# One more group of layer 1 by seven output products instead of eight, in a fused Fourier filter and two-layer MLP

## The chip, the cores and the metric

The kernel runs on one core of a Trainium2 chip. The metric is the device time of one execution in microseconds; three runs of the kernel before gave 1121.1 to 1121.34 us, median 1121.32. In the profile's names PE is TensorE (PEld its weight loads, which overlap the matmuls), DVE is VectorE, ACT is ScalarE, POOL is GpSimd, and SP issues most of the DMAs.

## The reference, cut to what matters

```python
X = np.fft.rfft(x, axis=1)                       # x: 2 x 3008 x 256
Yr = shrink(Xr @ w_r - Xi @ w_i + b_r)           # shrink: towards 0 by 0.01
Yi = shrink(Xr @ w_i + Xi @ w_r + b_i)
x = np.fft.irfft(Yr + 1j * Yi, n=3008, axis=1).reshape(6016, 256)
h = x @ w_in1;  x = (h * sigmoid(1.702 * h)) @ w_out1   # 256 -> 2048 -> 256, "layer 0"
h = x @ w_in2;  return (h * sigmoid(h)) @ w_out2        # the same sizes, "layer 1"
```

The change is in layer 1, and in the part of layer 0 that prepares layer 1's weights.

## The kernel before, in words

**Tiles.** The 6016 tokens lie in columns of `yt`, 256 features on 2 x 128 partitions. A layer goes through six blocks of tokens (five of 2 x 512 columns, the last of 2 x 448). In a block eight groups p = 0 to 7 follow each other, each for 256 of the 2048 hidden features, so a group's input part is a 2x2 by 2x2 product of 128-wide blocks. Every factor is held as a rounded high half (fp32r) and a low half, the remainder, and one product is three matmuls: high by high, and the two mixed ones. So the unit of PE's work is three matmuls.

**Scheme of seven.** The input part takes seven products instead of eight everywhere (`prod`, L1009 in `group`, L1191 in `group7`). The sums of input blocks that it needs are made once a block: two differences by `xsums` (L883, L884), then rounding (L898) and remainder (L905) by `xprep`. In groups 1 to 5 of layer 1 the output part takes seven products too (`s_prod`, L1127): its weights come ready split from DRAM (`stage` writes them in layer 0, `stream` loads 1 MB a group into `ring`), and its factors are the four gated values and the differences t1 = y3 - y1, t3 = b22 - y3, t2 = b22 - t1 (L1264 to L1266) and t4 = t2 - y4 (L1304). Groups 0, 6 and 7 use the plain eight products (`out7`, L1150), group 0 and 7 of them in `group`, not `group7`.

**Order in a group.** The engines run the order of the code. A group's own output products are taken by the next group, between its seven input products. In `group7` the input products are X (0, then 4, then 5, then 2 on one bank, with ACT or DVE reading in between), Y (1) and Z (3, then 6). ACT copies y1 (L1215), y2 (L1228) and y3 (L1230), DVE adds (L1219, L1244, L1246), ACT gates with Silu (L1201) and rounds (L1204), and the low half is subtracted by POOL (L1208; L1235 for factor 4) or by DVE (L1208, factor 2). Factor 3's low half goes by a DMA that adds (L1251). In the next group the output products come as factors 1, 2, 5, 7, 4, 6, 3; those of 5 and 4 go to the tile `r` and DVE adds them up (L1131, L1133), the others accumulate in banks. Factor 4 needs t4, which needs the y4 of the group before.

**Around a block's end.** In group 6 the sums of the seven are put together (`ends`). The four outputs of a block are added to the plain products of groups 6 and 7 by `final` (L1160) in group 0 of the next block, and DMAs issued by SP carry them off. SP also issues the loads of `ring`, one a group.

Of the kernel before, what the change touches and what calls it, by code (L numbers as in the profile page):

```python
# [21 lines left out]
P = 128  # L22
# [12 lines left out]
WEIGHTS += [(kind, 1, p, False) for kind in ("in", "out") for p in range(8)]  # L35
# [21 lines left out]
def spectral_mlp_kernel(ctx, tc, xin, mfwd, minv, wc, bias, w_in1, w_out1, w_in2, w_out2, outT):  # L57
# [186 lines left out]
    def stage(kind, p):  # L244
# [710 lines left out]
    def out_mm(l, i, p, row, h, gh, gl):  # L955
# [25 lines left out]
        if last:  # L981
            for mm in range(2):
                y = yt[:, mm, t0 + h * n : t0 + (h + 1) * n]
                (nc.scalar.copy if mm else nc.vector.tensor_copy)(y, acc[h, mm])
# [11 lines left out]
    def group(l, i, p, hook):  # L996
# [37 lines left out]
        (nc.vector.tensor_copy if (l, i, p) == (1, 0, 0) else nc.scalar.copy)(y1, X)  # L1034
# [80 lines left out]
    def s_prod(i, p, k):  # L1115
# [4 lines left out]
        one, first = k in (4, 5), p == seven(i)[0]  # L1120
        if k == 4 and p == seven(i)[-1]:
# [4 lines left out]
        for m, (st, mv) in enumerate(((a, hi), (z, hi), (a, lo))):  # L1126
            nc.tensor.matmul(t, st, mv, start=m == 0 and (one or first and k not in (2, 3)), stop=m == 2, skip_group_check=True)  # L1127
        if one:
            acc = accs[k][:, :n]
            if first and k == 5:  # L1130
# [6 lines left out]
    def out7(i, p, row, h, gh, gl):  # L1137
# [3 lines left out]
        for mm in range(2):  # L1141
            if p == 0 and row == h:
                for k in (C_BANK[h, mm],) + ((7,) if h and mm else ()):
                    banks[k] = ps_p[0].tile([P, 512], F32, tag="D", name="m3") if k == 3 else bank(1, f"m{k}")
            t = banks[C_BANK[h, mm]][:, :n]
            first = row == h and (p == 0 or p == tail and mm == 1)
# [4 lines left out]
        if p == 0 and row != h:  # L1151
            t = banks[C_BANK[h, 1]][:, :n]
            if h:
                nc.vector.tensor_copy(accs[6][:, :n], t)
            else:
                nc.scalar.mul(accs[4][:, :n], t, -1.0)
        if p == NPR - 1 and row != h:
            def final(mm):
                y = yt[:, mm, t0 + h * n : t0 + (h + 1) * n]
                nc.vector.tensor_add(y, home[("b22", "u", "w", "c22")[2 * h + mm]][:, :n], banks[C_BANK[h, mm]][:, :n])  # L1160
# [16 lines left out]
    def group7(i, p, hook):  # L1177
# [15 lines left out]
        def S(*ks):  # L1193
            for k in ks:
                if s7:
                    s_prod(i, p - 1, k)
                elif k in (1, 2, 7, 3):
                    out7_next()
# [16 lines left out]
        nc.scalar.copy(y1, X)  # L1215
# [9 lines left out]
        if ends:  # L1225
            u1, u2 = (home[x][:, :n] for x in ("b22", "u"))
# [20 lines left out]
        gate(b22, y2)  # L1247
        rounding(3, b22)
        if g7:
            nc.scalar.mul(factor(i, p, 3)[1], b22, -1.0)  # L1250
            nc.gpsimd.dma_start(out=factor(i, p, 3)[1], in_=b22, accum_op=ALU.add)  # L1251
        elif not ends:
            rest(nc.vector, 3, b22, (1, 1))
        if ends:
            add, sub = nc.vector.tensor_add, nc.vector.tensor_sub
            a4, a5, a6 = (accs[k][:, :n] for k in (4, 5, 6))
# [4 lines left out]
        gate(y3)  # L1261
# [13 lines left out]
        if ends:  # L1275
            add(a6, a6, a5)
            add(a5, u2, a5)
            if R3 == 1:
                rest(nc.vector, 3, b22, (1, 1))
                pend[-1], pend[-2] = pend[-2], pend[-1]  # L1280
            add(u2, u2, banks[7][:, :n])
# [34 lines left out]
    moves[0, last, 3].append(("out", 1, 0))  # L1316
# [28 lines left out]
    for at, f, x in (((1, 0, 2, 2), place_tail, 3), ((0, 5, 0, 2), put_aside, 3), ((0, 5, 7, 2), put_aside, 4), ((1, 0, 0, 2), place, 6), ((1, 0, 1, 2), place, 7), ((1, 1, 2, 3), put_back, 3), ((1, 2, 2, 3), put_back, 4)):  # L1345
# [29 lines left out]
    for at, (l, i, p) in enumerate(seq):  # L1375
# [55 lines left out]
        if (l, i, p) == (0, last, 0):  # L1431
            r = cv_p.tile([P, 2 * CU], mybir.dt.int64, tag="raw", name="raw64", bufs=1).bitcast(F32)
            raw64.extend((r[:, : 2 * CU], r[:, 2 * CU :]))
        if (l, i, p) == (1, 0, 0):
# [6 lines left out]
            ring[:] = [m_p.tile([P, MW], F32R, tag="m", name="ring")[:, : 2 * FS * D] for _ in range(2)][::-1]  # L1441
            home.update(zip(("t4", "u", "c22"), spots(3)), w=accs[5])
# [4 lines left out]
        if (l, i, p) == (1, 1, 1):  # L1447
            home.update(zip(("t4", "u", "c22"), spots(0)))
        if (l, i, p) == (1, 2, 1):
# [151 lines left out]
```

## Time and profile before

| | |
|---|---|
| median of three runs | 1121.32 us (1121.1 to 1121.34) |
| the profiled execution | 1124.35 us, of which its span 1122.6 us |
| PE, PEld busy | 1115.1 us (99%), 928.6 us (83%) |
| DVE, ACT, POOL busy | 841.1 us (75%), 831.8 us (74%), 582.1 us (52%) |
| TensorE clock granted | 1.0 of 2.4 GHz throughout |

Shares are averages over the Fourier part (to about 250 us), layer 0 (to about 650 us) and layer 1. A wait is read where it stands: in the idle time of PE's weight loads, and in the order of starts on the engines that make the operands.

### The profile page before, as it was taken

To read this page: it belongs to the slowest core of one execution; us is meant where nothing else is said; L and a number is where in the kernel's file an instruction comes from. 1 tells how busy PE (TensorE), PEld (TensorE's weight loads), DVE (VectorE), ACT (ScalarE), POOL (GpSimd) and SP (SyncE) were. 2 spreads that over 40 slices of the span, in tenths; PEclk is the share of its full clock that TensorE was granted. 3 is DMA by queue.
4 is the path that set the end of the run, shared out by engine and by line. 5 is a ranking of instruction groups with operands and counts; after the bars stand their busy time and mean duration, and the time that the engine had idled before them with its cause. 6 is when DMAs were issued, how large, how long until landed. Compare 5 with 4: busy or idle time off the path is not lost.

```text
span 1122.6 us, 15172 instructions
## 1 busy us (share of the span) xinstructions
PE 1115.1 (99%) x5000; PEld 928.6 (83%) x5000; DVE 841.1 (75%) x1264; ACT 831.8 (74%) x1567; POOL 582.1 (52%) x491
## 2 busy tenths in 40 slices
PE   9999999999999999999999999999999999999998
PEld 6878987888888888888889988888888888788897
DVE  7879997775575576676577787777887877878776
ACT  2488367876676677676678788778888788697785
POOL 0254056444443444434446647657657567477485
PEclk9999999999999999999999999999999999999999
DMA  8699586531121222312424444145054043242341
GB/s 335 167 174 210 148 158 119 118 73 38 38 76 38 54 59 80 108 48 84 120 87 158 153 150 105 47 160 141 10 197 113 19 153 102 76 140 57 121 138 41
DMA packets 54624, 123.87 MB, mean 110 GB/s; under 512 B 5265, under 2 KB 18193, under 8 KB 50578
## 3 DMA queue, kind: packets, MB, share of 16 engines
q1 hardware_dynamic: 36466, 92.44, 23.4%
q0 software_dynamic: 18080, 30.47, 16.9%
q8 instruction: 39, 0.64, 0.2%
q14 instruction: 39, 0.32, 0.1%
HBM read 71.85 MB, written 20.58 MB: 82 GB/s over the span
## 4 chain that ended last, share of the span: by engine, by line
PE 88%; DVE 4%; DMA 3%; issue 2%; ACT 2%; POOL 1%; SPq 0%; POOLq 0%; ACTq 0%; DVEq 0%
PE x L1009 24%; PE o L968 23%; PE x L1191 13%; PE m L1127 9%; PE m L1150 8%; PE r L1127 3%; PE psf L448 3%; PE y L1191 2%; DMA xl<-xt 2%; PE psf L489 1%; DMA x<-yt 1%; PE psm L642 1%; POOL xl L567 1%; DMA raw<-in_x 1%; PE psm L645 0%
## 5 line engine op out<-in xcount | busy, mean ns | idle before, releaser
L1022 POOL TENSOR_TENSOR g<-yt,g 128x512 fp32r<-128x512 f32 (+1 forms) x174 | 231.6, 1333 | 275.4 <-PE x L1009 129.5
L1009 PE MATMUL x<-x,wi 128*128 128x512 f32 (+1 forms) x1260 | 314.2, 387 | 1.4 <-ACT yt L1059 1.3
L968 PE MATMUL o<-g,wo 128*128 128x512 f32 (+1 forms) x1152 | 280.0, 385 | 0.0
L1009 PEld LDWEIGHTS x<-x,wi 128*128 128x128 f32 x1260 | 235.5, 188 | 49.9 <-ACT yt L1059 3.1
L968 PEld LDWEIGHTS o<-g,wo 128*128 128x128 f32 x1152 | 216.3, 188 | 40.3
L1208 POOL TENSOR_TENSOR g<-yt,g 128x512 fp32r<-128x512 f32 (+1 forms) x138 | 189.4, 1389 | 74.2 <-ACT g L1204 63.0
L1012 ACT ACTIVATE yt<-yt 128x512 f32<-128x512 f32 (+1 forms) x180 | 112.1, 623 | 133.7 <-DVE yt L1069 113.9
L1191 PE MATMUL x<-x,wi 128*128 128x512 f32 (+1 forms) x648 | 168.0, 385 | 0.1
L1017 ACT CAST g<-yt 128x512 fp32r<-128x512 f32 (+1 forms) x234 | 144.1, 616 | 6.0
L1191 PEld LDWEIGHTS x<-x,wi 128*128 128x128 f32 x648 | 121.5, 188 | 23.4 <-ACT yt L1230 0.8
L1127 PE MATMUL m<-g,ring 128*128 128x512 f32 (+1 forms) x414 | 111.7, 385 | 0.0
L1204 ACT CAST g<-yt 128x512 fp32r<-128x512 f32 (+1 forms) x186 | 108.0, 613 | 4.2 <-DVE yt L1266 1.1
L1150 PE MATMUL m<-g,wo 128*128 128x512 f32 (+1 forms) x396 | 97.9, 385 | 0.0
L188 POOL DMA_DIRECT2D cv_a<-cv_c x32 | 29.8, 930 | 125.4 <-DVE cv_c L187 105.1
L1127 PEld LDWEIGHTS m<-g,ring 128*128 128x128 f32 x414 | 77.7, 188 | 14.5
L1150 PEld LDWEIGHTS m<-g,wo 128*128 128x128 f32 x396 | 74.3, 188 | 13.9
L1201 ACT ACTIVATE yt<-yt 128x512 f32<-128x512 f32 (+1 forms) x108 | 67.0, 621 | 21.1 <-DVE yt L1244 17.0
L1039 DVE TENSOR_TENSOR yt<-yt,x 128x512 f32<-128x512 f32 (+1 forms) x60 | 40.3, 672 | 42.9 <-ACT yt L1034 42.8
L1069 DVE TENSOR_TENSOR yt<-yt,x 128x512 f32<-128x512 f32 (+1 forms) x60 | 40.4, 674 | 40.2 <-PE x L1009 39.9
L905 DVE TENSOR_TENSOR x<-yt,x 128x512 fp32r<-128x512 f32 (+1 forms) x55 | 47.6, 866 | 28.5 <-ACT x L898 28.4
L1022 DVE TENSOR_TENSOR g<-yt,g 128x512 fp32r<-128x512 f32 (+1 forms) x60 | 41.1, 685 | 31.7 <-ACT g L1017 31.7
L1133 DVE TENSOR_TENSOR raw<-raw,r 128x512 f32<-128x512 f32 (+1 forms) x48 | 32.5, 676 | 31.9 <-PE r L1127 31.9
(211 smaller groups left out, 1845.1 us busy)
## 6 DMA issues: line engine op xcount, KB each, us to landing
ring<-sout SPq DMA_DIRECT2D x30, 1024.0 KB, 5.9
raw<-in_wi SPq DMA_DIRECT2D x32, 256.0 KB, 3.8
cv_a<-cv_c POOLq DMA_DIRECT2D x32, 256.0 KB, 5.3
raw<-in_wo SPq DMA_DIRECT2D x16, 512.0 KB, 3.8
xl<-xt POOLq DMA_DIRECT2D x22, 256.0 KB, 7.1
out_t<-yt SPq DMA_DIRECT2D x20, 256.0 KB, 2.1
raw<-in_x SPq DMA_DIRECT2D x9, 512.0 KB, 6.4
ge<-yt POOLq DMA_DIRECT2D x15, 256.0 KB, 3.8
```

The lines of the kernel that those rows point to most:

```text
L905: E('xl1' if l else 'xl0' if i == 0 else 'xl', k).tensor_sub(lo, src, r32(hi))
L968: nc.tensor.matmul(acc[h, mm], st, mv, start=first and k == 0, stop=last and k == 2)
L1009: nc.tensor.matmul(ps, st, mv, start=first and m == 0, stop=m == 2, skip_group_check=True)
L1012: nc.scalar.activation(g, g if src is None else src, func)
L1017: nc.scalar.copy(gh, g)
L1022: eng.tensor_sub(gl, g, r32(gh))
L1127: nc.tensor.matmul(t, st, mv, start=m == 0 and (one or first and k not in (2, 3)), stop=m == 2, skip_group_check=True)
L1150: nc.tensor.matmul(t, st, mv, start=first and k == 0, stop=k == 2, skip_group_check=True)
L1191: nc.tensor.matmul(ps, st, mv, start=first and m == 0, stop=m == 2, skip_group_check=True)
L1201: nc.scalar.activation(g, g if src is None else src, AF.Silu)
L1204: nc.scalar.copy(factor(i, p, k)[0], src)
L1208: eng.tensor_sub(lo, src, r32(hi))
```

## The change

Group 0 of each block of layer 1 goes through `group7` and the scheme of seven, so seven output products instead of eight are taken in group 1. For that a sixth unit ("out", 0) is split and written to DRAM in layer 0, and `ring` is loaded six times a block instead of five. In group 0 the third difference t3 and factor 3's low half are made by POOL, t2 by DVE in group 1, and two of the four final sums move to group 1 as well. The two sums of `xsums` move from DVE in group 1 to POOL in group 6, and the seventh and fifth inputs (x 6, x 5) are rounded right after the sixth (x 4).

```diff
+WEIGHTS += [("in", 1, 6, False), ("in", 1, 7, False)] + [("out", 1, p, False) for p in range(6)]
...
     def seven(i):
-        return range(1, NPR - 2)
+        return range(NPR - 2)
-    STEPS = ((0, 4), (1, 2), (1, 3), (1, 7), (1, 5), (1, 5))
-    STAGED = {(3, 1): ("in", 6), (3, 3): ("in", 7), (4, 1): ("out", 1), (4, 3): ("out", 2), (5, 0): ("out", 3), (5, 2): ("out", 4), (5, 4): ("out", 5)}
+    STEPS = ((0, 1), (1, 2), (1, 3), (1, 7), (1, 5), (1, 5))
+    STAGED = {(2, 1): ("in", 6), (2, 3): ("in", 7), (3, 1): ("out", 0), (3, 3): ("out", 1), (4, 1): ("out", 2), (4, 3): ("out", 3), (5, 0): ("out", 4), (5, 3): ("out", 5)}
...
     def group7(i, p, hook):
...
         gate(b22, y2)
+        if p == 0:
+            gate(y3)
+        while p and finals:
+            finals.pop()()
         rounding(3, b22)
-        if g7:
+        if g7 and p:
             nc.scalar.mul(factor(i, p, 3)[1], b22, -1.0)
             nc.gpsimd.dma_start(out=factor(i, p, 3)[1], in_=b22, accum_op=ALU.add)
...
         if g7:
             nc.vector.tensor_sub(t1, y3, y1)
-            nc.vector.tensor_sub(t3, b22, y3)
-            nc.vector.tensor_sub(t2, b22, t1)
+            if len(finals) > 1:
+                finals.pop()()
+            if p == 0:
+                nc.gpsimd.tensor_sub(t3, b22, y3)
+                rest(nc.gpsimd, 3, b22)
+                after.append(lambda: nc.vector.tensor_sub(t2, b22, t1))
...
         if ends:
-            add(a6, a6, a5)
-            add(a5, u2, a5)
+            add(w12, u2, a5)
...
+            add(c22, w12, banks[7][:, :n])
             add(u2, u2, banks[7][:, :n])
...
+        def early():
+            rounding(5, t1)
+            rest(nc.gpsimd, 5, t1)
+            rounding(7, t3)
+            rest(nc.gpsimd, 7, t3)
+            later.append(lambda: (rounding(6, t2), rest(nc.gpsimd, 6, t2)))
...
         if g7:
             rest(nc.vector, 2, y4)
+            if finals:
+                finals.pop()()
             after.append(lambda: nc.vector.tensor_sub(home["t4"][:, :n], t2, y4))
-        put_off.append(third if g7 else fourth)
+        put_off.append((third if p else early) if g7 else fourth)
...
-                for x in ({1: (4,), 2: (6,), 3: (5,)} if (l, i) == (1, 0) else {1: (4,), 3: (6, 5)}).get(h, ()):
+                for x in ({1: (4,), 2: (6, 5)} if l else {1: (4,), 3: (6, 5)}).get(h, ()):
...
-            if h == (4 if l == 0 and i in (0, last - 1, last) else 1) and p == (NPR - 2 if l == 0 else 1) and (l, i) != (1, last):
-                xsums(*nxt)
+            if h == (5 if l else 4 if i in (0, last - 1, last) else 1) and p == NPR - 2 and (l, i) != (1, last):
+                xsums(*nxt, nc.gpsimd if l else nc.vector)
...
-        if l and 0 < p < NPR - 1:
+        if l and p < NPR - 1:
             group7(i, p, hook)
```

What this makes of the order is shown at three places. The first is PE in group 1 of block 1, where group 0's output products are taken (x and y are input products, m and r output products; `wi_5443` and `wi_5476` are the input weights of group 1). Before:

```order
L1191 MATMUL x<-x,wi_5443 128x512 x3
L1191 MATMUL y<-x,wi_5443 128x512 x3
L1150 MATMUL m_6753<-g,wo 128x512 x3
L1150 MATMUL m_6757<-g,wo 128x512 x3
L1191 MATMUL x<-x,wi_5443 128x512 x6
L1150 MATMUL m_6775<-g,wo 128x512 x3
L1150 MATMUL m_6779<-g,wo 128x512 x3
L1191 MATMUL x<-x,wi_5443 128x512 x6
L1150 MATMUL m_6775<-g,wo 128x512 x3
L1150 MATMUL m_6779<-g,wo 128x512 x3
L1191 MATMUL x<-x,wi_5443 128x512 x3
```

And now, in the same group:

```order
L1190 MATMUL x<-x,wi_5476 128x512 x3
L1190 MATMUL y<-x,wi_5476 128x512 x3
L1133 MATMUL m_6781<-g,ring 128x512 x3
L1190 MATMUL x<-x,wi_5476 128x512 x6
L1133 MATMUL m_6800<-g,ring 128x512 x3
L1133 MATMUL r<-g,ring 128x512 x3
L1190 MATMUL x<-x,wi_5476 128x512 x6
L1133 MATMUL m_6825<-g,ring 128x512 x3
L1133 MATMUL r<-g_6104,ring 128x512 x2
L1133 MATMUL r<-g_6105,ring 128x512
L1190 MATMUL x<-x,wi_5476 128x512 x3
L1133 MATMUL m_6843<-g,ring 128x512 x3
```

Eight plain products (six of them within the rows shown, the other two behind) become the seven of the scheme, with the two r products in their midst, the second of which reads factor 4 (`g_6104`, low half `g_6105`).

The second place is POOL from group 0 of block 2 into its group 1. Before (names `g_` with an even number are high halves, `ge` a borrowed tile; the last L1022 is y4's low half of group 0):

```order
L1022 TENSOR_TENSOR g_5985<-yt_1357,g_5984 128x512
L1022 TENSOR_TENSOR g_5991<-yt_1357,g_5990 128x512
L1022 TENSOR_TENSOR g_5993<-yt_1357,g_5992 128x512
L1208 TENSOR_TENSOR g_5985<-yt_1357,g_5984 128x512
L1251 DMA ge_6086<-yt_1357 128x512
```

And now, from the low half of factor 1 of group 0 to that of group 1:

```order
L1209 TENSOR_TENSOR g_6003<-yt_1357,g_6002 128x512
L1272 TENSOR_TENSOR yt_1357<-yt_1357 128x512
L1209 TENSOR_TENSOR g_6005<-yt_1357,g_6004 128x512
L1209 TENSOR_TENSOR g_6009<-yt_1357,g_6008 128x512
L1209 TENSOR_TENSOR g_6011<-yt_1357,g_6010 128x512
L1236 TENSOR_TENSOR g4_6105<-yt_1357,g4_6104 128x512
L1209 TENSOR_TENSOR g_6013<-yt_1357,g_6012 128x512
L1209 TENSOR_TENSOR g_6003<-yt_1357,g_6002 128x512
```

POOL makes t3 (L1272) and then the low halves of factors 3, 5, 7, 4, 6 and 1 in one row, where two subtractions stood behind factor 1's before.

The third place is DVE over the same stretch of block 2, from the y3 add of group 0 on (L1160, now L1159: final sums; L1022 and L1208, now L1209: low halves; L1219, now L1220: the y1 add). Before:

```order
L1074 TENSOR_TENSOR yt_1357<-yt_1357,x_7302 128x512
L1160 TENSOR_TENSOR yt_1357<-raw64_5210,m3_6775 128x512
L1160 TENSOR_TENSOR yt_1357<-yt_1357,m6_6779 128x512
L1022 TENSOR_TENSOR g_5987<-yt_1357,g_5986 128x512
L1160 TENSOR_TENSOR yt_1357<-yt_1357,m2_6753 128x512
L1160 TENSOR_TENSOR yt_1357<-yt_1357,m1_6757 128x512
L1219 TENSOR_TENSOR yt_1357<-yt_1357,y_7390 128x512
L883 TENSOR_TENSOR tmp_7409<-yt_1357 128x512
L884 TENSOR_TENSOR yt_1357<-yt_1357 128x512
L1244 TENSOR_TENSOR yt_1357<-yt_1357,x_7388 128x512
```

And now:

```order
L1247 TENSOR_TENSOR yt_1357<-yt_1357,x_7337 128x512
L1268 TENSOR_TENSOR yt_1357<-yt_1357 128x512
L1159 TENSOR_TENSOR yt_1357<-yt_1357,m1_6781 128x512
L1209 TENSOR_TENSOR g_6007<-yt_1357,g_6006 128x512
L1159 TENSOR_TENSOR yt_1357<-yt_1357,m2_6800 128x512
L1220 TENSOR_TENSOR yt_1357<-yt_1357,y_7423 128x512
L1274 TENSOR_TENSOR yt_1357<-yt_1357 128x512
L1327 TENSOR_TENSOR yt_1357<-yt_1357 128x512
L1137 COPY raw64_5244<-r_7461 128x512
L1245 TENSOR_TENSOR yt_1357<-yt_1357,x_7421 128x512
L1247 TENSOR_TENSOR yt_1357<-yt_1357,x_7422 128x512
L1159 TENSOR_TENSOR yt_1357<-yt_1357,m6_6843 128x512
```

Two final sums moved behind group 1's y3 add, t1 (L1268) came ahead of the first of them, and behind the y1 add stand t2 (L1274) and t4 (L1327) in place of the two input sums.

## Rows read from the trace of the kernel before

**Rows 1.** The page: span, and busy time of each engine.

```profile
span 1122.6 us, 15172 instructions
...
PE 1115.1 (99%) x5000; PEld 928.6 (83%) x5000; DVE 841.1 (75%) x1264; ACT 831.8 (74%) x1567; POOL 582.1 (52%) x491
```

**Rows 2.** The chain that ended last: start, us, what; 512, then 448 columns.

```profile
801.19 2.72 PE m L1150 x12
...
1114.10 4.88 PE m L1150 x24
```

**Rows 3.** Waits of PE's weight loads in layer 1: us in total, times, longest.

```profile
PEld x L1009 <- DVE x L905: 1.8, 5, 0.5
PEld x L1009 <- ACT yt L1059: 1.4, 5, 0.3
PEld x L1191 <- ACT yt L1230: 0.8, 2, 0.4
```

**Rows 4.** Timeline of PE, group 2 of block 1 (start, us, what).

```profile
749.35 0.84 PE L1191 MATMUL x<-x,wi 128*128 128x512 f32 x3
...
754.11 1.52 PE L1191 MATMUL x<-x,wi 128*128 128x512 f32 x6
```

**Rows 5.** Timeline of DVE, the same group.

```profile
751.65 1.71 DVE L1304 TENSOR_TENSOR yt<-yt 128x512 f32<-128x512 f32 x1
...
755.06 0.69 DVE L1244 TENSOR_TENSOR yt<-yt,x 128x512 f32<-128x512 f32 x1
755.74 0.69 DVE L1246 TENSOR_TENSOR yt<-yt,x 128x512 f32<-128x512 f32 x1
...
758.22 0.69 DVE L1264 TENSOR_TENSOR yt<-yt 128x512 f32<-128x512 f32 x1 [0.51 <-ACT yt L1201]
```

**Rows 6.** Timeline of ACT, the same group.

```profile
755.78 0.64 ACT L1201 ACTIVATE yt<-yt 128x512 f32<-128x512 f32 x1 [0.54 <-DVE yt L1244]
...
757.50 0.62 ACT L1201 ACTIVATE yt<-yt 128x512 f32<-128x512 f32 x1
758.02 0.58 ACT L1201 ACTIVATE yt<-x 128x512 f32<-128x512 f32 x1
758.63 0.62 ACT L1204 CAST g<-yt 128x512 fp32r<-128x512 f32 x1
...
760.27 1.14 ACT L1204 CAST g<-yt 128x512 fp32r<-128x512 f32 x2
```

**Rows 7.** Timeline of POOL, the same group.

```profile
751.52 3.00 POOL L1208 TENSOR_TENSOR g<-yt,g 128x512 fp32r<-128x512 f32 x2 [2.27 <-ACT g L1204]
754.48 1.30 POOL L1235 TENSOR_TENSOR g<-yt,g 128x512 fp32r<-128x512 f32 x1
755.74 2.56 POOL L1208 TENSOR_TENSOR g<-yt,g 128x512 fp32r<-128x512 f32 x2
...
760.99 1.28 POOL L1208 TENSOR_TENSOR g<-yt,g 128x512 fp32r<-128x512 f32 x1 [1.91 <-ACT g L1204]
```

**Rows 8.** Subtractions in SBUF, layer 1: count, busy us, mean ns; L1304's min/median/max.

```profile
L1304 DVE TENSOR_TENSOR yt<-yt 128x512 f32<-128x512 f32 x25 | 40.0, 1599 | 0.0
L1265 DVE TENSOR_TENSOR yt<-yt 128x512 f32<-128x512 f32 x25 | 17.1, 685 | 0.0
L1208 POOL TENSOR_TENSOR g<-yt,g 128x512 fp32r<-128x512 f32 x115 | 161.2, 1417 | 62.1 <-ACT g L1204 55.0 <-issue 6.9
...
L1304 DVE TENSOR_TENSOR yt<-yt x30: 1193/1586/1716, 672.5 to 1098.5; 128x512 f32<-128x512 f32 x25, 128x448 f32<-128x448 f32 x5
```

**Rows 9.** Layer 0: busy time of blocks 2 and 3, and weight loads' waits from 330 us.

```profile
332.40:414.00 81.60, 81.60 (x361) 67.55 (x360) 49.88 (x66) 55.76 (x102) 34.93 (x28) 1.00 0.20 52
414.00:495.60 81.60, 81.60 (x361) 67.51 (x361) 55.47 (x78) 58.23 (x106) 34.72 (x28) 1.00 0.28 81
...
PEld x L1009 <- DVE yt L1069: 0.4, 1, 0.4
```

In the first two: stretch, its length, then busy us of PE, PEld, DVE, ACT and POOL with their instructions, clock, DMA share and GB/s.

**Rows 10.** DMA issues on the page: count, KB each, us to landing.

```profile
ring<-sout SPq DMA_DIRECT2D x30, 1024.0 KB, 5.9
```

More of the change, by code (lines that the diff above doesn't have):

```diff
@@ L1033, in group @@
         prod(X, 0, 0)
-        (nc.vector.tensor_copy if (l, i, p) == (1, 0, 0) else nc.scalar.copy)(y1, X)
+        nc.scalar.copy(y1, X)
         while put_off:
@@ L1120, in s_prod @@
         one, first = k in (4, 5), p == seven(i)[0]
+        if first and not one:
+            banks[k] = ps_p[0].tile([P, 512], F32, tag="D", name="m3") if k == 3 else bank(1, f"m{k}")
         if k == 4 and p == seven(i)[-1]:
@@ L1126, in s_prod @@
         for m, (st, mv) in enumerate(((a, hi), (z, hi), (a, lo))):
-            nc.tensor.matmul(t, st, mv, start=m == 0 and (one or first and k not in (2, 3)), stop=m == 2, skip_group_check=True)
+            nc.tensor.matmul(t, st, mv, start=m == 0 and (one or first), stop=m == 2, skip_group_check=True)
         if one:
             acc = accs[k][:, :n]
-            if first and k == 5:
+            if first:
                 nc.vector.tensor_copy(acc, t)
@@ L1141, in out7 @@
         for mm in range(2):
-            if p == 0 and row == h:
-                for k in (C_BANK[h, mm],) + ((7,) if h and mm else ()):
-                    banks[k] = ps_p[0].tile([P, 512], F32, tag="D", name="m3") if k == 3 else bank(1, f"m{k}")
             t = banks[C_BANK[h, mm]][:, :n]
-            first = row == h and (p == 0 or p == tail and mm == 1)
+            first = row == h and p == tail and mm == 1
             a = w[:, 0, c % FS, mm * P : (mm + 1) * P]
@@ L1150, in out7 @@
                 nc.tensor.matmul(t, st, mv, start=first and k == 0, stop=k == 2, skip_group_check=True)
[L1151 to L1156, printed above, removed]
         if p == NPR - 1 and row != h:
+            held = [home[("u1", "u", "w", "c22")[2 * h + mm]][:, :n] for mm in range(2)]
             def final(mm):
                 y = yt[:, mm, t0 + h * n : t0 + (h + 1) * n]
-                nc.vector.tensor_add(y, home[("b22", "u", "w", "c22")[2 * h + mm]][:, :n], banks[C_BANK[h, mm]][:, :n])
+                nc.vector.tensor_add(y, held[mm], banks[C_BANK[h, mm]][:, :n])
                 o = outT[mm * P : (mm + 1) * P, t0 + h * n : t0 + (h + 1) * n]
@@ L1214, in group7 @@
         prod(X, 0, 0)
-        nc.scalar.copy(y1, X)
+        (nc.vector.tensor_copy if (i, p) == (0, 0) else nc.scalar.copy)(y1, X)
         while put_off:
@@ L1247, in group7 @@
         gate(b22, y2)
+        if p == 0:
+            gate(y3)
+        while p and finals:
+            finals.pop()()
         rounding(3, b22)
[L1249 removed]
+        if g7 and p:
             nc.scalar.mul(factor(i, p, 3)[1], b22, -1.0)
             nc.gpsimd.dma_start(out=factor(i, p, 3)[1], in_=b22, accum_op=ALU.add)
[L1252 to L1253 removed]
         if ends:
             add, sub = nc.vector.tensor_add, nc.vector.tensor_sub
[L1256 removed]
+            a4, a5 = (accs[k][:, :n] for k in (4, 5))
             add(u2, u1, banks[6][:, :n])
@@ L1260, in group7 @@
             rest(nc.vector, 3, b22, (1, 1))
-        gate(y3)
+        if p:
+            gate(y3)
         hook(7)
@@ L1390, in hook @@
                 stream(i, p + 1)
+            if h == 5 and more and nxt[0]:
+                stream(nxt[1], 0)
             if more:
@@ L1433, in spectral_mlp_kernel @@
             raw64.extend((r[:, : 2 * CU], r[:, 2 * CU :]))
+        if (l, i, p) == (0, last, NPR - 1):
+            ring[:] = [m_p.tile([P, MW], F32R, tag="m", name="ring")[:, : 2 * FS * D] for _ in range(2)]
         if (l, i, p) == (1, 0, 0):
@@ L1440, in spectral_mlp_kernel @@
             accs[5], accs[4] = raw64
-            ring[:] = [m_p.tile([P, MW], F32R, tag="m", name="ring")[:, : 2 * FS * D] for _ in range(2)][::-1]
-            home.update(zip(("t4", "u", "c22"), spots(3)), w=accs[5])
+            home.update(zip(("t4", "u", "c22", "u1"), spots(3)), w=m_p.tile([P, MW], F32, tag="m", name="more")[:, : 2 * CU])
             home.update(zip(("t1", "t2", "t3", "b22"), spots(4)))
```

39 lines of the change are left out of this document (24 added, 15 removed).

## Prediction, on record before the changed kernel was run

> **What bounds the kernel now.** The busy line comes first [rows 1]: PE is busy 99% of a span of 1122.6 us, DVE 75%, ACT 74%, POOL 52%. A busy PE says little by itself, so the chain of waits is read next [rows 2]: in layer 1 it runs matmul after matmul, twelve of 512 columns in 2.72 us and 24 of 448 columns in 4.88 us. That is 226.7 ns and 203.3 ns from one matmul to the next, three to a product, so 0.68 us a product. PE's weight loads wait 4.0 us in all of layer 1 [rows 3], so nearly every matmul removed shortens the run by its spacing, unless a new wait appears. A wait must come from the engines that prepare PE's operands. One group of seven is therefore followed engine by engine [rows 4 to 7], and last the one place where DVE and POOL disturb each other [rows 8].
>
> **What the change removes.** PE does 7 output products instead of 8 in group 0 of each block, three matmuls fewer in six blocks: 15 x 0.2267 + 3 x 0.2033 = 4.0 us. All of it lies on the path.
>
> The spacing of 226.7 ns is what these rows show [rows 2]. The Trainium skill ("TensorE: Matmul & The Clock Gate", Back-to-back issue gap) gives 512/2.4 + 2.5 = 216 ns for one isolated matmul and about 131 ns in a sustained stream; by these the saving would be an estimated 3.8 or 2.3 us. The rows decide, and the sum keeps 4.0.
>
> **The input factors at group 0.** Before, PE waits there for DVE's remainder of the seventh input (L905, five times, 1.8 us of weight-load idle) [rows 3]. Now its rounding and the fifth's stand on ACT ahead of the two product copies. Against this, the two sums for the next block go from DVE to POOL at the end of group 6. There two more POOL steps meet DVE's x remainders in group 7, and the five waits of PE for ACT's copy (1.4 us) can grow. A weight load runs ahead of its matmul, so less than the idle time is lost; I credit 0.6 us for both together, between a loss of 1 us and a gain of 1.8 us.
>
> **Staging and streaming.** One more unit (out 0) is split into seven in layer 0: eight passes of 128x128, two remainders on DVE, four DMAs on SP. The block with two staged units keeps DVE busy for 55.5 of 81.6 us, the one before it without any for 49.9, and over both and the rest of layer 0 weight loads wait once, for 0.4 us [rows 9]; the moved pair lands in that earlier block, whose conversions are as many. Cost 0, at most 1 us. Six more loads of 1 MB land in 5.9 us [rows 10]; each has a whole group (42 matmuls, 9.5 us) before PE asks for it. Cost 0; on SP they now queue behind two outputs instead of four. The final sums that move to group 1 hold banks 6 and 3; new products need these only at the group's end, 8.16 us in. Cost 0 while DVE reaches them in time.
>
> **What it adds in group 1 of each block.** This decides. Time u counts from the group's first matmul, at 0.68 per product: r5 (the product of factor 5) at 4.08, m7 at 6.12, r4 at 6.80, with the low half of factor 4 asked for by r4's third matmul, at 6.80 + 0.45 = 7.25.
>
> The lags come from a normal group. A product is added by DVE 0.95 after its first matmul (754.79 to 755.74), a gate follows the add's start by 0.72 (755.06 to 755.78), a DVE step the gate's start by 0.72 (757.50 to 758.22), a rounding its gate by 0.61 (758.02 to 758.63) [rows 4 to 6]. POOL takes a rounding up after 0.72 (760.27 to 760.99) [rows 6, 7].
>
> What a POOL step takes is read from start to start, 1.25 us (755.74 less 754.48 is 1.26) [rows 7]. DVE's steps stand 0.6 apart when nothing disturbs them. When both inputs lie in SBUF and POOL works, such a step takes 1.60 instead of 0.69 (L1304 against L1265), never over 1.72: it waits for the running POOL step and then goes in between two, and POOL's pair takes 3.00 instead of 2.56 [rows 5, 7, 8]. So the two alternate.
>
> The Trainium skill ("Perfetto Trace Analysis", GPSIMD Engine Instruction) calls POOL's spans unreliable and asks for start-to-start spacing. The span's mean of 1.42 us for L1208 [rows 8] would make the chain of five steps below 0.8 us longer, an estimated 5 us on the run; the trace agrees with the Trainium skill, since pairs stand 1.26 apart where DVE is silent. The lock itself is in the Trainium skill too ("SBUF — State Buffer", Who interferes with whom): the second to issue blocks until the first has finished. By its worst reading every one of DVE's three steps waits out a whole POOL step, which is the late order below.
>
> Now the chain, with group 0's last products (factor 6 of the input at u = -2.72, factor 5 at -0.68; between them and group 1 nothing else stands on PE):
> - y3 is added at -1.77 and gated at -1.05; y4 is gated at 0.20 and rounded at 0.81; roundings 5 and 7 start at 1.80 and 2.33.
> - DVE: t1 at -0.33, then a final sum, the low half of y4 (ready at 1.47), the second final sum, the y1 add, t2, t4. In the normal group t4 alone stands behind the y1 add.
> - POOL: t3 (held back by t1) 0.25 to 1.50, then the low halves of factors 3, 5, 7, 4, one behind the other. t3 and factor 3 are new here.
>
> DVE's step and POOL's next one fall due within 0.05 us of each other twice, so there is an early and a late order. **Early:** y4's low half 1.50, POOL factor 3 2.08 to 3.33, t2 to 3.91, POOL factor 5 to 5.16, t4 to 5.74, ACT rounds factor 4 at 5.9, POOL factor 7 to 6.99, factor 4 to 8.24. r5 waits 0.65 for its low half and r4 the rest: 8.24 + 0.06 - 7.25 = 1.05 us. **Late:** POOL first, factor 3 to 2.75, y4's low half to 3.33, POOL factor 5 to 4.58, t2 to 5.16, POOL factor 7 to 6.41, t4 to 6.99, ACT rounds factor 4 at 7.1, POOL 7.83 to 9.08: 1.9 us. If only one of the two ties goes to POOL, t4 still ends near 7, so three of four orders are late. In the normal group t4 ends at 4.0 and POOL is done with factor 4 at 6.4 [rows 4, 5, 7], 0.8 us before the deadline; two more POOL steps and two more DVE steps use more than that. By group 2 the lag is caught up.
>
> I take 1.5 us a block, between 1.05 and 1.9: 5 x 1.5 and 1.4 in the shorter last block, 8.9 us, bounds 6.2 and 11.3.
>
> **The sum:** -4.0 - 0.6 + 8.9 = +4.3 us. The profiled execution lasted 1124.35 us with its span of 1122.6, and becomes 1128.7; the median of the runs is 1121.32, which becomes 1125.6. I say 1125.5. From the bounds of the wait alone this case runs from 1122.9 to 1128.0.
>
> **Rivals.**
> 1. *The saving stands.* POOL or DVE is 0.6 us or more earlier than I have it (ACT's gates earlier, DVE before POOL each time), and PE waits under 0.4 us a block. For it: PE waits for POOL nowhere in layer 1 now [rows 3]. Against: POOL has five steps in a row from 0.25 on, whose last must end by 7.25, and DVE pushes three in between; 0.25 + 5 x 1.25 + 3 x 0.58 = 8.24 already. Time 1121.3 - 4.6 + 0 to 2.4: about 1117.5.
> 2. *The gap closes exactly.* The early order everywhere: -4.6 + 6.2 = +1.6, 1122.9, or a little less with a larger gain at group 0.
> 3. *Slower for another reason:* group 7. The two sums on POOL delay DVE's y1 add by one POOL step, and with it ACT's copy that the fifth product waits for. In the profile that copy is already late five times [rows 3]. It needs 0.7 us a block over today's to outweigh 4.0 us without any wait in group 1, and would then give 1122 to 1124; I see 0.2 us a block.
> 4. *The change doesn't do what it says:* excluded for PE, the built order has 18 matmuls fewer.
>
> **Chances.** Forecast (1123.6 to 1128.3) 0.46; the gap closes 0.26; the saving stands 0.24; group 7 decides 0.04. The bound of 0.2%, 2.2 us, is about what a measurement of this kernel can tell from no change. Faster by more: 0.24. Within: 0.26. Slower: 0.50, the forecast with group 7. The range that holds 8 in 10 must take in most of the rival with the saving: 1117.0 to 1128.5.
>
> **What would show it.** In the profile after: in group 1 of each block (the group with two copies of r on DVE) weight loads of r that wait for POOL or ACT, about 1 to 2 us together; t4 at 1.6 us and ending over 5.7 us into the group; POOL without a break from t3 to factor 1. Group 0 without the wait for L905's line. PE's sum of matmuls lower by 4.0 us. Wrong would be: spacing of 0.68 through group 1, with t4 done before 5 us; then the alternation of DVE and POOL is not as I read it.

## The result, and the profile of the changed kernel

The changed kernel takes **1133.1 us** (median of four runs, 1132.0 to 1134.6), the kernel before beside it 1121.2: a ratio of **1.0108** (95% interval 1.009 to 1.0125). That is slower by 12 us, outside the predicted range of 1117.0 to 1128.5. The profiled execution lasted 1134.58 us, with a span of 1132.8.

The page of the changed kernel, against [rows 1]:

```profile
span 1132.8 us, 15260 instructions
PE 1120.3 (99%) x4982; PEld 923.5 (82%) x4982; DVE 862.3 (76%) x1279; ACT 836.4 (74%) x1579; POOL 638.9 (56%) x524
```

PE has 18 matmuls fewer and is still busy 5 us longer, at the same 99%: this line does not tell where the time went. So the stages have to be measured. The table gives the summed length of layer 1's groups, from a group's first input product to the next group's first (every 21st matmul of the input products on PE's timeline; six blocks of groups 0 to 6, five of group 7). The last column is the stretch from the last block's group 7 to the end of the span.

```
us, summed over blocks        group 0   group 1   groups 2-6   group 7    end
before                          61.7      60.1       281.2       51.5     17.8
changed                         60.4      65.1       288.0       52.7     18.7
E1 ring loads later             60.3      64.9       280.6       51.1     18.9
E2 group 0 as the others        60.3      57.9       288.7       52.4     18.5
E3 both                         60.3      57.9       284.6       51.0     18.8
E8 both, and y's loads later    60.2      57.9       281.7       51.0     18.4
E9 before, ring loads later     60.9      60.1       280.6       51.0     17.8
```

Without any wait, group 1 of the changed kernel would take 60.1 - 4.0 = 56.1. It waits 9.0 us, and the prediction said 8.9. What the prediction did not have is in the next columns: groups 2 to 6, in which PE does the same matmuls as before, take 6.8 us more, group 7 1.2 us, and the end 0.9 us. By block, 4.4 of the 6.8 us lie in groups 4 and 6 of block 0 (11.16 and 11.24 us instead of 9.52 and 9.76) and in group 6 of block 1 (10.76 instead of 9.52), and 2.7 in groups 3, 4 and 6 of the last; blocks 2 to 4 lose nearly nothing there.

The section on the change leaves something out that bears on this. The change also moves DMA loads that SP issues: the input weights of groups 6 and 7 (`wi`, 0.9 MB each) from groups 0 and 1 of block 0 to groups 3 and 5, and the loads that bring y back for blocks 1 and 2 (1 MB each) from group 2 to group 6. SP runs ahead of these places. Before, it issued `wi` at 641.39 and 650.51 us and y 3.5 us into group 1; now it issues them at the starts of groups 3 and 5 of block 0 and of group 5 of blocks 1 and 2.

**Group 1** of block 3 begins at 899.76. PE, then DVE and POOL (start, us, what; the idle time ahead in brackets), against the normal group in [rows 4, 5, 7]:

```profile
904.37 0.93 PE L1133 MATMUL r<-g,ring 128*128 128x512 f32 x3 [0.37 <-DVE yt L1220]
907.27 0.70 PE L1133 MATMUL r<-g,ring 128*128 128x512 f32 x2
908.60 0.50 PE L1133 MATMUL r<-g,ring 128*128 128x512 f32 x1 [0.62 <-POOL g L1236]
```

```profile
901.24 1.78 DVE L1209 TENSOR_TENSOR g<-yt,g 128x512 fp32r<-128x512 f32 x1 [0.58 <-ACT g L1205]
903.55 0.67 DVE L1220 TENSOR_TENSOR yt<-yt,y 128x512 f32<-128x512 f32 x1
904.86 1.67 DVE L1327 TENSOR_TENSOR yt<-yt 128x512 f32<-128x512 f32 x1
...
899.42 1.80 POOL L1272 TENSOR_TENSOR yt<-yt 128x512 f32<-128x512 f32 x1 [1.30 <-ACT yt L1202]
901.18 4.79 POOL L1209 TENSOR_TENSOR g<-yt,g 128x512 fp32r<-128x512 f32 x3
907.26 1.28 POOL L1236 TENSOR_TENSOR g<-yt,g 128x512 fp32r<-128x512 f32 x1 [1.28 <-ACT g L1235]
```

POOL runs without a break from t3 to factor 7, DVE's low half of y4 and t4 take 1.78 and 1.67 us, t4 ends at 906.53, 6.77 us into the group, and r4's last matmul waits for factor 4. ACT is held up too: its rounding of factor 4 waits for t4, and the gate of b22 (the value that becomes factor 3) stands behind that rounding in the program. It starts 9.03 us into the group, where a normal group has it at 6.43 [rows 4, 6]:

```profile
906.56 0.62 ACT L1235 CAST g<-yt 128x512 fp32r<-128x512 f32 x1 [2.61 <-DVE yt L1327]
...
908.79 0.63 ACT L1202 ACTIVATE yt<-yt 128x512 f32<-128x512 f32 x1
```

Over the blocks t4 ends at 5.60, 6.93, 5.77, 6.77, 6.76 and, with 448 columns, 6.04; the group is 0.95, 1.89, 1.12, 1.73, 1.71 and 1.54 us too long. These are the early order (5.74, 1.05) and the late one (6.99, 1.9) of the prediction.

**The later groups.** What ACT waited for in layer 1 (us in total, times, longest), and the landing of factor 3's DMA in the same stretch, in the changed kernel:

```profile
ACT yt L1202 <- DMA g<-yt: 17.8, 10, 3.1
ACT yt L1202 <- DMA ge<-yt: 8.3, 7, 1.5
...
DMA to landing us min/median/max: 3.1/7.2/9.0
```

and in the kernel before:

```profile
ACT yt L1201 <- DMA g<-yt: 4.0, 3, 1.6
...
DMA to landing us min/median/max: 3.1/4.0/7.9
```

The waiting instruction is the gate that writes b22. The DMA of the group before still reads b22. Two POOL rows, two SP rows and one ACT row of the changed kernel (block 1, groups 3 and 4) show the loop:

```profile
760.91 0.88 POOL L1256 DMA_DIRECT2D g<-yt  x1 [0.19 <-issue]
770.52 0.88 POOL L1256 DMA_DIRECT2D ge<-yt  x1
...
761.09 0.33 SPq L1114 DMA_DIRECT2D ring<-sout  x1
770.61 0.32 SPq L1114 DMA_DIRECT2D ring<-sout  x1
...
768.41 0.63 ACT L1202 ACTIVATE yt<-yt 128x512 f32<-128x512 f32 x1 [1.12 <-DMA g<-yt]
```

The DMA is issued 0.18 us ahead of a ring load and lands 7.4 us later, at 768.32. The gate that waits for it starts at 768.41, and its own DMA follows at 770.52, 2.1 us on, 0.09 us ahead of the next ring load. 7.4 + 2.1 is 9.5 us, just a group: so the late order renews itself. In the kernel before the same two issues lie 0.83 us apart, and the DMA lands after 4.0:

```profile
758.23 0.84 POOL L1251 DMA_DIRECT2D g<-yt  x1
...
759.06 0.33 SPq L1110 DMA_DIRECT2D ring<-sout  x1
```

The late order alone costs PE little: blocks 2 to 4 have it in many of their groups and lose nearly nothing in groups 2 to 6. Where one of the moved loads comes in behind the ring load, the DMA takes longer than the loop allows. In block 1 SP also brings 1 MB of y back at 780.57 (L1355), and the chain runs through the DMA:

```profile
779.91 8.55 DMA g<-yt
788.46 0.02 issue
...
788.54 0.64 ACT yt L1202
```

In block 0 the loads of `wi` do the same. The DMA ahead of the first lands after 9.00 us, the DMA ahead of the second (698.35, 0.61 us ahead) after 8.99, and groups 4 and 6 are the long ones:

```profile
677.76 0.88 POOL L1256 DMA_DIRECT2D g<-yt  x1 [0.55 <-ACT g L1255]
...
677.89 0.32 SPq L1114 DMA_DIRECT2D ring<-sout  x1
678.26 0.42 SPq L1359 DMA_DIRECT2D wi<-sin  x1
```

In block 2, group 4, where the early order is back, y's load comes too, and the DMA lands after 4.04 us:

```profile
859.57 0.86 POOL L1256 DMA_DIRECT2D g<-yt  x1
...
860.47 0.32 SPq L1114 DMA_DIRECT2D ring<-sout  x1
860.96 0.56 SPq L1355 DMA_DIRECT2D yt<-y  x1
```

So these losses take both, the late order and the moved load. The changed kernel with these loads where they were was not run.

Over all kernels, in blocks of 512 columns, the landing follows the lead over the ring load: 4.0 us with a lead of 0.83 to 0.90 us, 4.9 to 5.8 with 0.69 to 0.75, 6.2 to 7.2 with 0.59 to 0.66, 7.0 to 8.0 with 0 to 0.54 (once 5.4 and once 9.9), about 3.3 in most cases with no load near, 8.5 to 9.0 with a late order and a moved load as well. Five landings with a lead of 0.84 to 0.90 took 6.8 to 7.9 us all the same; in each a packet of the instruction queue was in flight beside the two, as in one that took 4.0. Whether that packet is the cause was not tried. The Trainium skill ("DMA: Bandwidth & Descriptors", Issuing engines are not separate DMA queues) says that DMAs of all engines run on the same 16 DMA engines and interleave; these landings agree with it.

### The profile page after: what moved, and what is told of

It reads as the page before. It is cut to its first block, busy times and chain, and to the rows that moved or that the text cites. A ratio compares the mean times of both kernels' runs of the same rounds, so it can differ in the third digit from the quotient of the medians.

```text
span 1132.8 us, 15260 instructions
## 1 busy us (share of the span) xinstructions
PE 1120.3 (99%) x4982; PEld 923.5 (82%) x4982; DVE 862.3 (76%) x1279; ACT 836.4 (74%) x1579; POOL 638.9 (56%) x524
## 4 chain that ended last, share of the span: by engine, by line
PE 75%; DVE 7%; DMA 7%; ACT 5%; issue 4%; POOL 3%; DVEq 0%; POOLq 0%; ACTq 0%
PE o L969 23%; PE x L1013 21%; PE x L1190 10%; PE m L1133 7%; PE m L1153 4%; DMA g<-yt 3%; PE psf L449 3%; PE r L1133 2%; PE y L1190 2%; PE psf L490 1%; POOL g L1209 1%; DMA ge<-yt 1%; ACT yt L1202 1%; ACT g L1205 1%; DMA xl<-xt 1%
## 5 line engine op out<-in xcount | busy, mean ns | idle before, releaser
L1026 POOL TENSOR_TENSOR g<-yt,g 128x512 fp32r<-128x512 f32 (+1 forms) x156 | 206.5, 1326 | 230.5 <-PE x L1013 128.3
L1209 POOL TENSOR_TENSOR g<-yt,g 128x512 fp32r<-128x512 f32 (+1 forms) x168 | 240.3, 1449 | 58.8 <-ACT g L1205 54.1
L1133 PE MATMUL m<-g,ring 128*128 128x512 f32 (+1 forms) x504 | 137.3, 387 | 0.5 <-POOL g L1209 0.4
L1021 ACT CAST g<-yt 128x512 fp32r<-128x512 f32 (+1 forms) x210 | 129.2, 615 | 5.0
L1205 ACT CAST g<-yt 128x512 fp32r<-128x512 f32 (+1 forms) x222 | 129.2, 612 | 3.8
L1133 PEld LDWEIGHTS m<-g,ring 128*128 128x128 f32 x504 | 94.4, 188 | 20.9 <-POOL g L1209 2.3
L1202 ACT ACTIVATE yt<-yt 128x512 f32<-128x512 f32 (+1 forms) x126 | 77.9, 619 | 36.1 <-DMA g<-yt 17.8
L1073 DVE TENSOR_TENSOR yt<-yt,x 128x512 f32<-128x512 f32 (+1 forms) x54 | 36.4, 673 | 42.6 <-PE x L1013 41.6
L1043 DVE TENSOR_TENSOR yt<-yt,x 128x512 f32<-128x512 f32 (+1 forms) x54 | 36.3, 673 | 42.0 <-ACT yt L1038 42.0
L906 DVE TENSOR_TENSOR x<-yt,x 128x512 fp32r<-128x512 f32 (+1 forms) x55 | 51.6, 945 | 16.3 <-ACT x L899 16.2
L1133 PE MATMUL r<-g,ring 128*128 128x512 f32 (+1 forms) x198 | 58.0, 395 | 4.9 <-POOL g L1236 2.4
L1153 PE MATMUL m<-g,wo 128*128 128x512 f32 (+1 forms) x252 | 62.0, 386 | 0.0
L1268 DVE TENSOR_TENSOR yt<-yt 128x512 f32<-128x512 f32 (+1 forms) x36 | 26.1, 726 | 44.4 <-ACT yt L1202 42.9
L1026 DVE TENSOR_TENSOR g<-yt,g 128x512 fp32r<-128x512 f32 (+1 forms) x54 | 36.8, 682 | 29.6 <-ACT g L1021 29.6
```

The source lines that it names most:

```text
L906: E('xl1' if l else 'xl0' if i == 0 else 'xl', k).tensor_sub(lo, src, r32(hi))
L1021: nc.scalar.copy(gh, g)
L1026: eng.tensor_sub(gl, g, r32(gh))
L1133: nc.tensor.matmul(t, st, mv, start=m == 0 and (one or first), stop=m == 2, skip_group_check=True)
L1153: nc.tensor.matmul(t, st, mv, start=first and k == 0, stop=k == 2, skip_group_check=True)
L1202: nc.scalar.activation(g, g if src is None else src, AF.Silu)
```

## The experiments

**E1. Ring loads issued later, on ACT's queue.**

```diff
-            if l == 1 and h == 5 and p + 1 in seven(i):
-                stream(i, p + 1)
+            if l == 1 and h == 2 and p > 1 and p in seven(i):
+                stream(i, p, nc.scalar)
```

> The changed kernel, with the 1 MB loads of the streamed weights (rings 2 to 5 of a block and ring 0 of the next) issued from ACT's queue ahead of the copy of y2 in the group itself, some 2.5 us into it, instead of by SP at the end of the group before (0.19 us into the group). Nothing else moves. Theory A (the second loss is a collision: the accumulating DMA of factor 3, 4.0 us when it runs alone, takes 7 to 9 us when a ring load is issued at the same moment; the gate of the next group waits for it, issues its own DMA 2.1 us later, and so meets the next ring load too): the landing of the factor 3 DMA goes back to about 4 us in groups 2 to 5, gates no longer wait 26 us for it, and the time falls by the 6 to 7 us that groups 3 to 6 are too long in blocks 0, 1 and 5, from 1133.1 to about 1126.5. Group 1 of each block keeps its 0.95 to 1.9 us. Theory B (the lag of group 1 itself is carried on, the DMA is only a bystander): landings shorten, the time stays within 2 us of 1133.

Measured 1125.93 us (ratio to before 1.0036, 1.0024 to 1.0048): 4.2 us over the kernel before beside it instead of 11.9, so 7.7 us gone. The DMA lands after 3.3 us in the median, and the gate waited for it once, for 0.3 us. Groups 2 to 7 lose all their excess, group 1 keeps its 8.8. Theory A holds: the second loss is a collision of transfers. But that nothing else moves, as I expected, is not so. Without the ring loads in its queue SP issued `wi` at the start of group 0 and y's loads in groups 1 and 2, so this run took the moved loads out of the late order too and can't tell the two apart; E6 and E7 below can, for the ring loads. The edit also changes two things about the ring loads themselves, the queue and the time; that the landing falls with the lead while all ring loads stay on SP (5.2 us at 0.69 in E4, 7.1 at 0.51 in E5) speaks for the time.

What is left lies within 0.5 us of the predicted 1125.5. That is partly luck: the edit also spares the 1.4 us that the kernel before loses to the same collision (E9), and the end of the run, for which the prediction had no term, costs about 1 us more.

**E2. Group 0 as the other groups have it; E3. both edits.**

```diff
-        if g7 and p:
+        if g7:
             nc.scalar.mul(factor(i, p, 3)[1], b22, -1.0)
...
-            if p == 0:
-                nc.gpsimd.tensor_sub(t3, b22, y3)
-                rest(nc.gpsimd, 3, b22)
-                after.append(lambda: nc.vector.tensor_sub(t2, b22, t1))
-            elif p == seven(i)[-1]:
+            if p == seven(i)[-1]:
```

> The changed kernel, with group 0 of each block as the other groups of seven have it: the third difference on DVE instead of GpSimd, the second difference right behind it, and the low half of factor 3 by ACT's multiplication and the accumulating DMA instead of a GpSimd subtraction. Two long POOL steps and one step of the DVE that alternates with them leave the stretch ahead of factor 4. By the working of the prediction t4 then ends about 4.5 us into group 1 instead of 5.7 to 7.0, POOL ends factor 4 at about 7.2 of a deadline of 7.25, and the wait in group 1 falls from 8.9 us in all to 0 to 2 us. Theory A (the late DMAs of factor 3 come from that lag, by way of a collision that keeps itself going): they go too, and the time falls by 14 us, to about 1118 to 1120. Rival (the collision has a cause of its own, such as the six more ring loads): only group 1 gains, about 1125.

> Both edits together: ring loads on ACT's queue, and group 0 with the third difference on DVE and factor 3 by DMA. If the two losses are separate and both edits take theirs away whole: 1133.1 - 8.9 - 6.8 = 1117.4. If the collision is only a consequence of the lag in group 1, this is the same as the kernel with the second edit alone, within 1 us. If issuing loads from ACT costs something of its own, it shows here as a time above that kernel's.

E2 measured 1129.95 us, E3 1122.98. In E2 group 1 waits 1.8 us instead of 9.0 (1.1 of it in block 3), as the prediction's working has it, but groups 2 to 6 stay over 7 us too long, so both expectations for the time fell. Taking the wait of PE out of group 1 does not bring the DMA back to its place: in block 1 it is still issued 0.2 us ahead of the ring load, and lands after 9.9 us. There t4 still ends 4.75 us into group 1 instead of the normal group's 4.0 [rows 4, 5], since a final sum stands ahead of the y1 add, and ACT's gate of b22 starts at 7.02 instead of 6.43. E3 misses its 1117.4 by 5.6: 1.8 us are what group 1 still waits, 0.9 lie in the last block (below), and 3.2 in groups 2 and 3 of block 1. With the ring loads gone from its queue, SP reached the load of y early, in group 1, and the factor 3 DMA issued 0.8 us behind it took 10.6 us (the expectation of E8 below calls these loads 2 MB each; the profile has 1 MB):

```profile
745.71 10.59 DMA ge<-yt
...
756.38 0.64 ACT yt L1202
```

**E4. A delay in group 1 of the kernel before.**

```diff
+        for _ in range(3 * (p == 1)):
+            nc.scalar.copy(y2, y2)
         gate(b22, y2)
```

> The kernel before, with three more copies on ACT (y2 onto itself, 0.6 us each by the spacing of its copies, 1.6 to 1.8 us together) ahead of the gate of b22 in group 1 of each block, and nowhere else. In the kernel before that gate's DMA is issued 8.8 to 9.2 us into a group, 0.9 us ahead of the ring load. Theory A (capture): a delay of 1.6 us in one group puts the DMA of that group beside the ring load, it lands after 7 us or more instead of 4.0, the next gate waits for it, and the late order holds through groups 2 to 5 of some blocks: landings of 7 us and more in most groups, gates that wait for the DMA in 10 or more groups instead of 3, although nothing in those groups was changed. Theory B (the lag is worked off in a group or two): landings are back at 4 us from group 3 on. The time itself rises by 1 to 10 us under either, since the copies delay group 1 as well; the landings decide.

Measured 1132.91 us, with a median landing of 3.8 and two waits of the gate. This does not show capture: PE waited the delay out in group 2 of each block (11.2 instead of 9.52 us), and was on time afterwards. But it hardly tests it either, since in the kernel before no ring load starts at the end of group 1. In group 2 the lead was still 0.69 to 0.75 us in the five longer blocks, the DMA landed after 4.9 to 5.7, and one group later the lead was back at 0.88 or more: a lag of this size is worked off. The delay belonged in group 2 itself.

**E5, E6. One copy, and two, in group 2 of the kernel before; E7. two copies, with the ring loads later.** The edit is E4's with `p == 2`, and in E7 E1's for p over 2.

> The kernel before, with one more copy on ACT (y2 onto itself, 0.53 us from its start to the next) ahead of the gate of b22 in group 2 of each block, nowhere else. The three copies in group 1 tried first could not test the collision: in the kernel before no ring load starts at the end of group 1, the delayed DMA landed in 3.3 us, and PE waited the lag out in group 2. At the end of group 2 a ring load does start, 0.83 us after the DMA of that group is issued. Theory A (collision that keeps itself going): one copy brings the DMA to some 0.3 us ahead of the ring load; it lands after about 7.3 us instead of 4.0, and the DMAs of groups 3 to 5, where nothing is changed, land after 7 us too, since a gate that waits for a landing issues the next DMA 2.1 us later: 7.3 + 2.1 is 9.4 of a group's 9.52 us. Median landing of this DMA in the run 6 us or more; the time 2 to 6 us above before. Theory B (lag is worked off): landing 7 in group 2 at most, 4.0 from group 3 on; time within 2 us of before.

> The same with two copies (1.06 us). Theory A: the DMA of group 2 is issued 0.2 us behind the ring load, lands after 7 to 9 us, and the late order holds in groups 3 to 5; the time 4 to 10 us above before, of which the copies' own delay is at most 1.06 us in each of six blocks. Theory B: the delay is paid once in each block, at most 6 us, and landings from group 3 on are 4.0 us.

> The kernel before with the two copies in group 2, and the ring loads 3 to 5 of each block issued from ACT's queue ahead of the copy of y2 in the group itself, some 2.5 us into it, instead of by SP at 0.19 us. Theory A: without a ring load beside it the delayed DMA lands after 3.3 to 4.0 us, no gate waits for it, and what is left is what the copies cost by themselves, 0 to 1 us a block: between 1120.5 and 1126, below the run with two copies and the loads on SP by as much as that one lost to the collision. Theory B: no difference between the two.

E5 measured 1123.45 us, E6 1127.48, E7 1121.89. Factor 3's DMA in E5, E6 and E7, in this order:

```profile
DMA to landing us min/median/max: 3.1/6.3/8.0
...
DMA to landing us min/median/max: 3.1/6.8/8.0
...
DMA to landing us min/median/max: 3.1/3.3/5.1
```

In E5 the DMA of group 2 is issued 0.3 us later than before and lands after 7.0 to 7.5 us in every block. In blocks 0 to 2 it gains 0.1 to 0.2 us a group and is back at its 8.82 us into the group by group 4 or 5; in blocks 3 to 5 the late order holds to group 4, although in blocks 3 and 4 the kernel before has a landing of over 7 us in group 4 too. In E6 the DMAs of groups 2 to 4 land after 6.2 to 8.0 us in every block. E7 has the same two copies, and no gate waits for a DMA at all: 5.6 us less than E6. In E6 and E7 `wi` and y are loaded where the kernel before loads them, so these 5.6 us are the ring loads' alone. Theory A holds with the limit that a small lag can be worked off, slowly. That a lag in group 2 is enough, in a kernel that is otherwise the one before, shows that neither the sixth ring load nor POOL's work nor the moved loads are needed for a loss of this kind, only the meeting.

**E8. E3 with the loads of y on ACT's queue too, in group 6; E10. the same again; E9. the kernel before with the ring loads later alone.**

```diff
-        nc.sync.dma_start(out=yt[:, :, t0 : t0 + TB], in_=aside[i])
+        nc.scalar.dma_start(out=yt[:, :, t0 : t0 + TB], in_=aside[i])
```

> The changed kernel with ring loads on ACT's queue, group 0 with the third difference on DVE and factor 3 by DMA, and now also the two 2 MB loads that bring y back issued from ACT's queue in group 6 of blocks 1 and 2, where the program has them, instead of by SP, which reaches them in group 1 of block 1 once the ring loads no longer stand ahead of them (8.82 us into it; the factor 3 DMA issued 0.8 us later took 10.6 us, and groups 2 and 3 of that block were 1.45 and 1.73 us longer). If that collision is all that is special in block 1: 3.2 us less than without this edit, 1123.0 - 3.2 = 1119.8. If not: 1123.

> The kernel before with nothing changed but ring loads 3 to 5 of each block issued from ACT's queue ahead of the copy of y2 in the group itself. It tells how much of the gain of the kernel with three edits comes from the ring loads alone. In the kernel before, the DMA of factor 3 meets a ring load late in some blocks (landing 7 us and more in group 4 or 5 of three blocks; group 6 and 7 there are 0.2 to 0.6 us longer), about 1.3 us in all. Theory A (scheme of seven for p = 0 is worth its 4.0 us once the two losses are gone, and the moved loads only remove collisions): 1121.4 - 1.3 = 1120, above the kernel with three edits by 1 us or more. Rival (the three edits' gain is the ring loads' alone): 1119, the same as that kernel.

> The kernel with three edits once more, beside the one above on the same chip, in five rounds: 1118 to 1120 and 1 to 2 us under the kernel before with the ring loads moved.

E8 measured 1119.07 us (ratio 0.998, 0.9969 to 0.9991), E10 1118.85 (0.9974, 0.9965 to 0.9984), E9 1120.5 (0.9987, 0.9977 to 0.9996). The version with three edits is the fastest of all, 0.2 to 0.3% under the kernel before. About 1.3 us of that come from the ring loads alone, and 1.7 from the seven products of group 0: 4.0 saved and 0.6 at group 0, less 1.8 of wait in group 1, 0.9 in the last block and 0.2 in block 1's group 2. The end, 0.5 us longer than in E9, is not in this sum, so it does not close to better than half a microsecond.

**E11. E8 with t3 on POOL and t2 on DVE behind the y1 add; E12. E8 with factor 3 on POOL.**

```diff
+            if p == 0:
+                nc.gpsimd.tensor_sub(t3, b22, y3)
+                after.append(lambda: nc.vector.tensor_sub(t2, b22, t1))
```

```diff
+            if p == 0:
+                rest(nc.gpsimd, 3, b22)
```

> The kernel with three edits, with one half of the group 0 edit undone: the third difference is on GpSimd again, and the second on DVE behind the y1 add, as in the changed kernel; factor 3 stays with ACT's multiplication and the DMA. One long POOL step is out of the chain ahead of factor 4 (its DMA issue takes 0.9 us instead of 1.25 and alternates with nothing), the DVE steps stand as in the changed kernel. By the working of the prediction t4 ends 0.6 to 1.25 us earlier than in the changed kernel and group 1 waits 0.3 to 0.9 us a block instead of 1.5: 1119 + 2 to 5 = 1121 to 1124. If only the number of POOL steps mattered it would be 1119 to 1121, if only the DVE steps mattered 1126.

> The other half undone: factor 3 by a GpSimd subtraction again, the third and second differences on DVE in group 0. POOL makes factors 3, 5, 7, 4; the third difference no longer holds it back, so factor 3 can start at about 0.25 us and factor 5 at 1.8 when ACT has rounded it. By the working of the prediction the chain is one POOL step shorter and DVE has one step less behind the y1 add: group 1 waits 0 to 0.6 us a block, 1119 to 1122.5.

E12 measured 1121.08 us, with 5.0 us of wait in group 1, 0.6 in most blocks. E11 measured **1146.26**, 20 us over the worst that I expected. Its group 1 is 30 us too long in all. DVE and POOL in block 1:

```profile
742.66 4.34 DVE L1209 TENSOR_TENSOR g<-yt,g 128x512 fp32r<-128x512 f32 x1 [0.89 <-ACT g L1205]
...
741.79 0.88 POOL L1256 DMA_DIRECT2D g<-yt  x1 [2.51 <-ACT g L1255]
742.39 1.60 POOL L1272 TENSOR_TENSOR yt<-yt 128x512 f32<-128x512 f32 x1
743.76 2.68 POOL L1209 TENSOR_TENSOR g<-yt,g 128x512 fp32r<-128x512 f32 x2
```

DVE's low half of y4, issued during POOL's t3, ends only after three POOL steps. It takes 4.0 to 4.6 us in five blocks (3.8 for t2 in the sixth). DVE did not get in between the steps at all, and PE's weight loads waited up to 3.0 us for it. So neither part alone is harmless, and t3 on POOL with factor 3 by DMA is by far the worse of the two. It is also far worse than both parts together, which cost 8.8 us in E1.

## Why the prediction was wrong, point by point

- **Saving, 4.0 us:** right. 18 matmuls fewer; group 1's undisturbed length is 9.52 us instead of 10.20.
- **Group 0 and group 7, -0.6 us:** right, once the collision is taken out on both sides. Group 0 gains 1.3 us over the blocks (1.4 in E1), but 0.8 of that is what the kernel before loses there to late DMAs, since E9 has 60.9. From E9 to E1 it is 0.6, and group 7 is the same within 0.1. The 1.2 us that group 7 loses in the changed kernel go with E1's edit, so they are the collision's; the third rival had no part.
- **Staging, 0:** holds. Layer 1 begins at 647.1 to 650.5 us in the eight profiles with the changed layer 0, at 648.0 to 650.3 in the six with the old one.
- **Group 1, 8.9 us:** right, at 9.0, with both orders seen. One link was another: r5 did not wait for its low half, which POOL had done at 904.19 in the trace, before r5's third matmul asks for it. It waited for its bank, which DVE's late y1 add was still reading (the 0.37 above). The price was the same. How the blocks split between the two orders, two early and three late of 512 columns, was not predicted; that the middle of the two came out so well is partly luck.
- **"The two alternate", never over 1.72 us [rows 8]:** nearly right for the changed kernel (up to 1.82), wrong as a rule. E3 has a t4 of 2.35 us, E11 4.34. The Trainium skill ("SBUF — State Buffer", Who interferes with whom) says that the second to issue blocks until the first instruction is done. E11's DVE step blocked for three.
- **"By group 2 the lag is caught up": this step failed.** I followed group 1's lag as far as PE and stopped there. ACT's rounding of factor 4 waits for the late t4 (2.61 us in block 3), the gate of b22 behind it is late by as much, its DMA comes within 0.2 us of the ring load, and from there the lag feeds itself: 17.8 and 8.3 us of waits for this DMA in layer 1 instead of 4.0, and 8.0 us in groups 2 to 7.
- **"Ring loads, cost 0": failed with it.** I asked whether a load arrives in time for PE, which it does (5.9 us [rows 10] of 9.5), and not what it does to the other transfer in flight. Nor did I price the loads of `wi` and y, which the change moves into the stretch where the DMAs are late; 4.4 of the 6.8 us lie right behind them. The kernel before held a hint that I did not use: three of its gates waited 4.0 us in all for this DMA, whose longest landing was 7.9 us against a median of 4.0. (That one had a lead of 0.90 us and a packet of the instruction queue beside it.)
- **The end of the run, no term:** 18.7 us from the last group 7 on instead of 17.8, and 18.1 to 18.9 in all kernels with the change against 17.8 to 18.0 without. What makes it longer was not looked into.

The sum with the missing terms: 1121.2 - 4.0 - 1.3 + 9.0 + 6.8 + 1.2 + 0.9 = 1133.8; measured 1133.1. It can't be closer than the start of layer 1 allows, which varies by 2 to 3 us between profiles with the same layer 0. The 8.0 us of groups 2 to 7 are what E1 took away, 7.7 on the clock.

## What to carry to other kernels

When a change makes one step late, follow it to every DMA that it issues, and look what else is issued within a microsecond there: a buffer that is rewritten while a slow DMA still reads it ties one round to the next, and a round that is late by landing time plus turnaround stays late. Give two transfers of a round places half a round apart, by what they wait for, not by their order on a queue that runs ahead. And a load taken off a queue lets the one behind it go early (E1, E3): move both, or the experiment changes two things.

## What the runs showed that I had not expected

- A 256 KB accumulating DMA within SBUF lands in 3.3 us alone, mostly 4.0 with a lead of 0.9 us over a 1 MB load, 7.0 to 8.0 with a lead under 0.5: the last 0.4 us of lead are worth 3 us of landing.
- A DVE step with both inputs in SBUF waited out three POOL steps in E11 (4.34 us), where in the changed kernel it went in after one (1.78). In E11 the steps stand right behind a DMA issue on POOL; whether that decides it was not tried.
- With 448 columns, the matmuls of the last block run at one of two spacings through whole groups, 8.51 us or 8.68 us for the same 42 (202.6 or 206.7 ns each), with no wait between them: 8.51 in E12, 8.68 in E8, at a granted clock of 1.0. What chooses is open; it is worth 0.9 us here.
